# Half-token units and four PSUM sets in the up-projection of a GeGLU kernel

## The chip, the cores and the metric

The kernel runs on one core of a Trainium2 chip. The metric is the device time of one execution in microseconds: the median of six runs is 316.26 us, with runs from 314.55 to 317.0 us. A profile of one further execution shows where its time goes.

## What is computed

The input x has 32 x 32 = 1024 tokens of 1024 numbers; w_gate and w_up are 1024 x 3584, w_down is 3584 x 1024; all are bf16.

```
def _gelu(x):
    return jax.nn.gelu(x, approximate=True)

def reference(x, w_gate, w_up, w_down):
    return (_gelu(x @ w_gate) * (x @ w_up)) @ w_down
```

## The kernel before

The program is written engine by engine, with explicit semaphores. Each function (prog_sp, prog_act, prog_pool, prog_pe, prog_dve) is the instruction list of one engine in its order. `wait(clock, value)` makes an engine wait until another engine or a DMA has counted up to a value; a wait that is already known to hold is left out. The lists are written by hand; nothing plans or reorders them.

**Up-projection.** The 3584 hidden columns are 28 chunks m of 128. For each chunk TensorE forms the gate product G and the up product U for all 1024 tokens, hidden columns on the partitions: 2 products x 2 token halves h (512 tokens each) x 8 steps dk over the 1024 input columns, 32 matmuls of 128x128 by 128x512 (L292). The eight PSUM banks are two sets of four: two banks for G, two for U; chunk m uses set m % 2 (L287). A set is free again when D3 of chunk m - 2 is done (L274). Normally the order is G h0, G h1, U h0, U h1. For chunk 0 alone the order follows the arrival of x (L275 to L280): for each piece of x the four G steps and the four U steps that it allows.

**Between the two projections.** ScalarE and VectorE work a chunk of 1024 tokens at a time: A1 (L334) squares G into t; D1 (L352) forms i = (t + 1) * G; A2 (L337) takes the sigmoid of i; D2 (L357) multiplies it by U; D3 (L360) multiplies by G and writes hT, in bf16, to SBUF. D2 waits for the end of U. t, i and the result of D2 have two buffers each.

**Down-projection.** For each of 8 token blocks tc and two column halves dh TensorE sums 28 matmuls over m in one bank (L313). dh = 0 is copied out by ScalarE (L343), dh = 1 by VectorE (L366), and SP stores each block (L251).

**Loads.** x arrives transposed: SP issues four DMA transposes (L230), of 512 tokens by 512 columns each, in the order (h, q2) = (0,0), (0,1), (1,0), (1,1). The weights w_gate and w_up come in groups of chunks of sizes 1, 1, 2, 3, 4, 4, 4, 4, 4, 1, into two buffers each (wg0, wg1, wu0, wu1). The queues are:

- ACT issues wg of groups 0 and 1, behind one small activation that loads its table (L323, L326).
- POOL issues all wu loads (L217): those of groups 0 and 1 at once, those of groups 2 and 3 as soon as the transposed piece (0,1) has landed, the later ones when the chunk that last used the buffer has been read.
- SP issues wg from group 2 on (L242), behind its four transposes, the later ones with the same waits.
- wd arrives in seven groups of four chunks, by turns from SP and POOL (L201), each behind the G of a given chunk.

TensorE waits for wg and wu of a group at the group's first chunk, and within chunk 0 for the piece of x that a matmul reads (L289). Ahead of chunk 0 it runs eight dummy matmuls on a memset tile (L263).

Of the kernel before, what the change touches and what calls it, by code (L numbers as in the profile page):

```python
# [6 lines left out]
P = 128  # L7
BF16 = mybir.dt.bfloat16
FP32 = mybir.dt.float32
ACTF = mybir.ActivationFunctionType  # L10
ALU = mybir.AluOpType
# [77 lines left out]
def bass_standalone__geglu_ffn__sampling_kernel(  # L89
# [46 lines left out]
    NWB = 2  # L136
# [3 lines left out]
    wd_gate_chunk = [min(FM - 1, 3 + 3 * k) for k in range(len(wd_groups))]  # L140

# [9 lines left out]
    Q_X = {(h, q2): _Clock(f"x{h}{q2}", 16) for h in range(2) for q2 in range(2)}  # L151
# [10 lines left out]
    with ExitStack() as es:  # L162
# [8 lines left out]
        t_bufs = [sb("tb0", [P, N], FP32), sb("tb1", [P, N], FP32)]  # L171
        i_bufs = [sb("ib0", [P, N], FP32), sb("ib1", [P, N], FP32)]
        su_bufs = [sb("sb0", [P, N], FP32), sb("sb1", [P, N], FP32)]
# [8 lines left out]
        def g_full(s):  # L182
            return ps[:, 4 * s:4 * s + 2, :].rearrange("p a b -> p (a b)")

        def u_full(s):
            return ps[:, 4 * s + 2:4 * s + 4, :].rearrange("p a b -> p (a b)")
# [9 lines left out]
        def issue_wd(ew, eng, mine, upto_chunk, clock, force=False):  # L196
            for k in list(mine):
                if force or wd_gate_chunk[k] <= upto_chunk:
                    ew.wait(C_PE, ctx.get(("G", wd_gate_chunk[k])))
                    a, b = wd_groups[k]  # L200
                    ew.do(lambda: eng.dma_start(wd[:, a:b, :], wd_r[:, a:b, :]), clock=clock)  # L201
                    mine.remove(k)

        def prog_pool(eng):
            pool = _Eng(ctx, eng, C_POOL)
            ctx.set("scr", pool.do(lambda: eng.memset(osb[:, 0, 0:512], 1.0)))  # L206
            wd_mine = [k for k in range(len(wd_groups)) if k % 2 == 1]
            known_chunk = -1
            for j in range(NG):
                c0, gsz, buf, slot0 = groups[j]  # L210
                if j == 2:
                    pool.wait(Q_X[(0, 1)], ctx.get(("x", 0, 1)))
                if group_war[j] is not None:
                    pool.wait(C_PE, ctx.get(("U", group_war[j])))
                    known_chunk = max(known_chunk, group_war[j])
                ctx.set(("wu", j), pool.do(
                    lambda: eng.dma_start(wdst(wu_bufs, j), wsrc(wu_r, j)),  # L217
                    clock=Q_WU[j]))
                if j >= 2:
                    issue_wd(pool, eng, wd_mine, known_chunk, Q_WD_POOL)  # L220
            issue_wd(pool, eng, wd_mine, FM, Q_WD_POOL, force=True)
            ctx.set("wd_pool_total", Q_WD_POOL.n)

        XPIECES = [(0, 0), (0, 1), (1, 0), (1, 1)]

        def prog_sp(eng):
            sp = _Eng(ctx, eng, None)
            for (h, q2) in XPIECES:
                ctx.set(("x", h, q2), sp.do(
                    lambda: eng.dma_start_transpose(  # L230
                        xT[:, 4 * q2:4 * q2 + 4, h * 512:(h + 1) * 512],
                        xf[h * 512:(h + 1) * 512, q2 * 512:(q2 + 1) * 512],
                    ), clock=Q_X[(h, q2)]))
            wd_mine = [k for k in range(len(wd_groups)) if k % 2 == 0]
            known_chunk = -1
            for j in range(2, NG):
                c0, gsz, buf, slot0 = groups[j]
                if group_war[j] is not None:
                    sp.wait(C_PE, ctx.get(("U", group_war[j])))
                    known_chunk = max(known_chunk, group_war[j])  # L240
                ctx.set(("wg", j), sp.do(
                    lambda: eng.dma_start(wdst(wg_bufs, j), wsrc(wg_r, j)),  # L242
                    clock=Q_WG[j]))
                issue_wd(sp, eng, wd_mine, known_chunk, Q_WD_SP)
            issue_wd(sp, eng, wd_mine, FM, Q_WD_SP, force=True)
            ctx.set("wd_sp_total", Q_WD_SP.n)
            last = None
            for tc in range(TC):
                for dh in range(DH):
                    sp.wait(C_ACT if dh == 0 else C_DVE, ctx.get(("E", tc, dh)))  # L250
                    last = sp.do(lambda: eng.dma_start(  # L251
                        out_r[:, tc, dh * 512:(dh + 1) * 512],
                        osb[:, tc, dh * 512:(dh + 1) * 512]), clock=Q_OUT)
            sp.wait(Q_OUT, last)

        NDUMMY = 8

        def prog_pe(eng):
# [6 lines left out]
            ctx.set("dummy", v)  # L265
            pe.wait(C_PE, v)
            for m in range(FM):
                j, buf, slot = chunk_info[m]
                s = m % 2
                if m == groups[j][0]:  # L270
                    pe.wait(Q_WG[j], ctx.get(("wg", j)))
                    pe.wait(Q_WU[j], ctx.get(("wu", j)))
                if m >= 2:
                    pe.wait(C_DVE, ctx.get(("D3", m - 2)))  # L274
                if m == 0:  # L275
                    order = []
                    for (h, q2) in XPIECES:
                        for key in ("G", "U"):
                            for dk in range(4 * q2, 4 * q2 + 4):
                                order.append((key, h, dk))  # L280
                else:
                    order = [(key, h, dk) for key in ("G", "U") for h in range(NH)
                             for dk in range(DK)]
                cnt = {"G": 0, "U": 0}
                for (key, h, dk) in order:
                    wb = (wg_bufs if key == "G" else wu_bufs)[buf]
                    bank = 4 * s + (0 if key == "G" else 2) + h  # L287
                    if m == 0:
                        pe.wait(Q_X[(h, dk // 4)], ctx.get(("x", h, dk // 4)))  # L289
                    cnt[key] += 1  # L290
                    last = (cnt[key] == NH * DK)
                    v = pe.do(lambda: eng.matmul(  # L292
                        ps[:, bank, :],
                        wb[:, dk, slot * P:(slot + 1) * P],
                        xT[:, dk, h * 512:(h + 1) * 512],
                        start=(dk == 0), stop=(dk == DK - 1),
                    ), mark=last)
                    if last:
                        ctx.set((key, m), v)
            pe.wait(C_DVE, ctx.get(("D3", FM - 2)))  # L300
            pe.wait(Q_WD_SP, ctx.get("wd_sp_total"))
            pe.wait(Q_WD_POOL, ctx.get("wd_pool_total"))
            for tc in range(TC):
                for dh in range(DH):
                    b = (tc % 4) * 2 + dh
                    if tc >= 4:
                        pe.wait(C_ACT if dh == 0 else C_DVE, ctx.get(("E", tc - 4, dh)))
                    v = None
                    for m in range(FM):
                        if m == FM - 1:  # L310
                            pe.wait(C_DVE, ctx.get(("D3", FM - 1)))
# [9 lines left out]
        def prog_act(eng):  # L321
            act = _Eng(ctx, eng, C_ACT)
            act.do(lambda: eng.activation(warm[:, 0:1], const0, ACTF.Sigmoid))  # L323
            for j in range(2):
                ctx.set(("wg", j), act.do(
                    lambda: eng.dma_start(wdst(wg_bufs, j), wsrc(wg_r, j)),  # L326
                    clock=Q_WG[j]))
            for m in range(FM):
                s = m % 2
                tb, ib = t_bufs[m % 2], i_bufs[m % 2]  # L330
                act.wait(C_PE, ctx.get(("G", m)))
                if m >= 2:
                    act.wait(C_DVE, ctx.get(("D2", m - 2)))
                ctx.set(("A1", m), act.do(lambda: eng.activation(  # L334
                    tb[:, :], g_full(s), ACTF.Square, scale=SQ_SCALE)))
                act.wait(C_DVE, ctx.get(("D1", m)))
                ctx.set(("A2", m), act.do(lambda: eng.activation(  # L337
                    tb[:, :], ib[:, :], ACTF.Sigmoid, scale=SIG_SCALE)))
# [7 lines left out]
        def prog_dve(eng):  # L346
            dve = _Eng(ctx, eng, C_DVE)
            for m in range(FM):
                s = m % 2
                tb, ib, sub = t_bufs[m % 2], i_bufs[m % 2], su_bufs[m % 2]  # L350
                dve.wait(C_ACT, ctx.get(("A1", m)))
                ctx.set(("D1", m), dve.do(lambda: eng.scalar_tensor_tensor(  # L352
                    out=ib[:, :], in0=tb[:, :], scalar=1.0, in1=g_full(s),
                    op0=ALU.add, op1=ALU.mult)))
                dve.wait(C_ACT, ctx.get(("A2", m)))
                dve.wait(C_PE, ctx.get(("U", m)))
                ctx.set(("D2", m), dve.do(lambda: eng.tensor_tensor(  # L357
                    sub[:, :], tb[:, :], u_full(s), ALU.mult)))
                dve.wait(C_DVE, ctx.get(("D2", m)))
                ctx.set(("D3", m), dve.do(lambda: eng.tensor_tensor(  # L360
                    hT[:, m, :], sub[:, :], g_full(s), ALU.mult)))
# [57 lines left out]
```

## Time and profile before

| | us |
|---|---|
| median of six runs | 316.26 |
| the profiled execution, whole | 312.07 |
| its span, first to last instruction | 310.3 |
| TensorE busy with matmuls | 297.6 |
| VectorE busy | 108.1 |
| ScalarE busy | 64.5 |

The span is the time from the first to the last instruction of the profiled execution; the execution's own time has 1.77 us around that. The page has rows of 40 slices, each 7.76 us long: a digit is the busy share of an engine in tenths, and PEclk the granted clock of TensorE in tenths. A line of the chain gives the start, the length and what the chain runs through. A line of a group gives, behind the bar, the busy time and the mean ns of one instruction, then the idle time ahead of it and what ended it. Matmuls are pipelined, so a group's length on TensorE is somewhat more than the distance to the next group's start; the distance of starts is what one uses for the cost of a matmul.

### The profile page before, as it was taken

To read this page: it belongs to the slowest core of one execution; us is meant where nothing else is said; L and a number is where in the kernel's file an instruction comes from. 1 tells how busy PE (TensorE), PEld (TensorE's weight loads), DVE (VectorE), ACT (ScalarE), POOL (GpSimd) and SP (SyncE) were. 2 spreads that over 40 slices of the span, in tenths; PEclk is the share of its full clock that TensorE was granted. 3 is DMA by queue.
4 is the path that set the end of the run, shared out by engine and by line. 5 is a ranking of instruction groups with operands and counts; after the bars stand their busy time and mean duration, and the time that the engine had idled before them with its cause. 6 is when DMAs were issued, how large, how long until landed. Compare 5 with 4: busy or idle time off the path is not lost.

```text
span 310.3 us, 2978 instructions
## 1 busy us (share of the span) xinstructions
PE 297.6 (96%) x1352; PEld 133.3 (43%) x1352; DVE 108.1 (35%) x92; ACT 64.5 (21%) x66; POOL 12.0 (4%) x18
## 2 busy tenths in 40 slices
PE   4759999999999999999999999999999999999996
PEld 1224444444444444444444444444444444444442
DVE  0006555445545555455455554553000000000000
ACT  1013222233232222332332223321000000000000
POOL 3200010020001002000200100000000000000000
PEclk9589999999999999999999999999999999999999
DMA  7991009138008302900780150000100010010001
GB/s 169 219 302 53 2 3 346 59 112 293 0 2 271 135 2 62 343 2 2 226 316 2 28 174 0 2 0 0 35 18 17 17 36 17 17 35 18 17 17 34
DMA packets 25900, 26.40 MB, mean 85 GB/s; under 512 B 12080, under 2 KB 21296, under 8 KB 25888
## 3 DMA queue, kind: packets, MB, share of 16 engines
q1 hardware_dynamic: 21056, 15.21, 16.8%
q0 software_dynamic: 2752, 10.49, 9.9%
q10 hardware_dynamic: 2080, 0.52, 0.8%
q8 instruction: 10, 0.16, 0.2%
q14 instruction: 2, 0.02, 0.0%
HBM read 22.02 MB, written 2.10 MB: 78 GB/s over the span
## 4 chain that ended last, share of the span: by engine, by line
PE 92%; SPq 4%; DMA 3%; DVE 0%; issue 0%
PE ps L292 61%; PE ps L313 31%; SPq L230 4%; DMA xT<-in_x_dram 3%; DVE osb L366 0%
## 5 line engine op out<-in xcount | busy, mean ns | idle before, releaser
L292 PE MATMUL ps<-xT,wg 128*128 128x512 bf16 x448 | 104.1, 385 | 8.5 <-DMA wu<-in_w_up_dram 5.1
L292 PE MATMUL ps<-xT,wu 128*128 128x512 bf16 x448 | 103.5, 384 | 0.0
L313 PE MATMUL ps<-wd,hT 128*128 128x512 bf16 x448 | 96.9, 379 | 0.0
L292 PEld LDWEIGHTS ps<-xT,wg 128*128 128x128 bf16 x448 | 44.2, 99 | 63.5 <-issue 8.4
L292 PEld LDWEIGHTS ps<-xT,wu 128*128 128x128 bf16 x448 | 44.3, 99 | 54.2 <-issue 2.5
L313 PEld LDWEIGHTS ps<-wd,hT 128*128 128x128 bf16 x448 | 43.8, 98 | 52.9
L352 DVE SCALAR_TENSOR_TENSOR ib<-tb,ps 128x1024 f32<-128x1024 f32 x28 | 34.2, 1222 | 75.0 <-ACT tb L334 75.0
L334 ACT ACTIVATE tb<-ps 128x1024 f32<-128x1024 f32 x28 | 28.7, 1024 | 114.1 <-PE ps L292 114.1
L357 DVE TENSOR_TENSOR sb<-tb,ps 128x1024 f32<-128x1024 f32 x28 | 34.2, 1221 | 34.8 <-PE ps L292 33.6
L337 ACT ACTIVATE tb<-ib 128x1024 f32<-128x1024 f32 x28 | 29.6, 1057 | 36.1 <-DVE ib L352 36.1
L366 DVE CAST osb<-ps 128x512 bf16<-128x512 f32 x8 | 5.5, 692 | 89.3 <-PE ps L313 89.3
L360 DVE TENSOR_TENSOR hT<-sb,ps 128x1024 bf16<-128x1024 f32 x28 | 34.2, 1221 | 1.0
L343 ACT ACTIVATE osb<-ps 128x512 bf16<-128x512 f32 x8 | 4.8, 597 | 86.6 <-PE ps L313 86.6
L217 POOL DMA_DIRECT2D wu<-in_w_up_dram x10 | 9.0, 900 | 164.9 <-PE ps L292 155.5
L263 PE MATMUL ps<-osb 128*128 128x512 bf16 x8 | 3.2, 578 | 1.3 <-POOL osb L206 1.3
L263 PEld LDWEIGHTS ps<-osb 128*128 128x128 bf16 x8 | 1.0, 141 | 3.0 <-issue 1.7
L201 POOL DMA_DIRECT2D wd<-in_w_down_dram x3 | 2.3, 762 | 0.0
L323 ACT ACT_TABLE_LOAD x1 | 1.3, 1283 | 0.7 <-PEq L404 0.7
L206 POOL MEMSET osb<- 128x512 bf16 x1 | 0.5, 525 | 0.3 <-POOLq L404 0.3
L323 ACT ACTIVATE warm<-const-float32-0.0 128x1 f32<-128x1 f32 x1 | 0.2, 203 | 0.0
L404 POOL MEMSET const-float32-0.0<- 128x1 f32 x1 | 0.1, 99 | 0.2 <-issue 0.2
L404 POOL MEMSET const-float32-1.0<- 128x1 f32 x1 | 0.1, 99 | 0.0
(2 smaller groups left out, 0.2 us busy)
## 6 DMA issues: line engine op xcount, KB each, us to landing
wg<-in_w_gate_dram SPq DMA_DIRECT2D x5, 1024.0 KB, 5.4
wu<-in_w_up_dram POOLq DMA_DIRECT2D x5, 1024.0 KB, 10.0
wd<-in_w_down_dram SPq DMA_DIRECT2D x4, 1024.0 KB, 10.9
wd<-in_w_down_dram POOLq DMA_DIRECT2D x3, 1024.0 KB, 10.8
out_dram<-osb SPq DMA_DIRECT2D x16, 128.0 KB, 1.7
wu<-in_w_up_dram POOLq DMA_DIRECT2D x3, 256.0 KB, 7.8
wu<-in_w_up_dram POOLq DMA_DIRECT2D x1, 768.0 KB, 8.2
wg<-in_w_gate_dram SPq DMA_DIRECT2D x1, 768.0 KB, 10.4
```

What stands on the lines that cost most here:

```text
L217: lambda: eng.dma_start(wdst(wu_bufs, j), wsrc(wu_r, j)),
L230: lambda: eng.dma_start_transpose(xT[:, 4 * q2:4 * q2 + 4, h * 512:(h + 1) * 512], xf[h * 512:(h + 1) * 512, q2 * 512:(q2 + 1) * 512],), c ...
L263: v = pe.do(lambda: eng.matmul(ps[:, 7, :], osb[:, 0, 0:P], osb[:, 0, 0:512], start=True, stop=True), mark=(i == NDUMMY - 1))
L292: v = pe.do(lambda: eng.matmul(ps[:, bank, :], wb[:, dk, slot * P:(slot + 1) * P], xT[:, dk, h * 512:(h + 1) * 512], start=(dk == 0), stop ...
L313: v = pe.do(lambda: eng.matmul(ps[:, b, :], hT[:, m, tc * P:(tc + 1) * P], wd[:, m, dh * 512:(dh + 1) * 512], start=(m == 0), stop=(m == F ...
L334: ctx.set(("A1", m), act.do(lambda: eng.activation(tb[:, :], g_full(s), ACTF.Square, scale=SQ_SCALE)))
L337: ctx.set(("A2", m), act.do(lambda: eng.activation(tb[:, :], ib[:, :], ACTF.Sigmoid, scale=SIG_SCALE)))
L343: ctx.set(("E", tc, dh), act.do(lambda: eng.activation(osb[:, tc, dh * 512:(dh + 1) * 512], ps[:, b, :], ACTF.Copy)))
L352: ctx.set(("D1", m), dve.do(lambda: eng.scalar_tensor_tensor(out=ib[:, :], in0=tb[:, :], scalar=1.0, in1=g_full(s), op0=ALU.add, op1=ALU.m ...
L357: ctx.set(("D2", m), dve.do(lambda: eng.tensor_tensor(sub[:, :], tb[:, :], u_full(s), ALU.mult)))
L360: ctx.set(("D3", m), dve.do(lambda: eng.tensor_tensor(hT[:, m, :], sub[:, :], g_full(s), ALU.mult)))
L366: ctx.set(("E", tc, dh), dve.do(lambda: eng.tensor_copy(osb[:, tc, dh * 512:(dh + 1) * 512], ps[:, b, :])))
```

## The change

The unit of work in the up-projection becomes one chunk for one token half, written (m, h), with 16 matmuls. The order of units is (0,0), (1,0), (0,1), (1,1), then h = 0 and h = 1 of each further chunk. The eight PSUM banks become four sets of two, one bank for G and one for U; unit u uses set u % 4 and waits for D3 of the unit four before it. ScalarE and VectorE work unit by unit, on 512 tokens, with four buffers each for t, i and the result of D2, each 512 wide. The x transposes become eight pieces of 512 tokens by 256 columns, and chunks 0 and 1 both follow the pieces. The loads of groups 0 to 3 change their queues: ACT issues wg0, wu0, wg1, wu1; SP issues wg2, wu2, wg3, wu3 behind a wait for the last piece of x; POOL begins with group 4. The waits of the wd loads are for the end of U in place of G. In the down-projection each block waits for the last unit of its bank's set and, chunk by chunk, for D3 of the second token half. There are seven dummy matmuls in place of eight. The diff, with the parts that only rename left out:

```diff
+    NXQ = 4
+    QW = DK // NXQ
+    XPIECES = [(h, q2) for h in range(NH) for q2 in range(NXQ)]
+
+    units = [(0, 0), (1, 0), (0, 1), (1, 1)]
+    for m in range(2, FM):
+        for h in range(NH):
+            units.append((m, h))
+    NU = len(units)
+    NSETS = 4
...
+        NTB = 4
+        t_bufs = [sb(f"tb{i}", [P, 512], FP32) for i in range(NTB)]
+        i_bufs = [sb(f"ib{i}", [P, 512], FP32) for i in range(NTB)]
+        su_bufs = [sb(f"sb{i}", [P, 512], FP32) for i in range(NTB)]
...
+        def gbank(u):
+            return 2 * (u % NSETS)
+
+        def ubank(u):
+            return 2 * (u % NSETS) + 1
...
-                    ew.wait(C_PE, ctx.get(("G", wd_gate_chunk[k])))
+                    ew.wait(C_PE, ctx.get(("U", wd_gate_chunk[k], 1)))
...
+        def load_w(ew, eng, which, j):
+            if which == "wg":
+                return ctx.set(("wg", j), ew.do(
+                    lambda: eng.dma_start(wdst(wg_bufs, j), wsrc(wg_r, j)), clock=Q_WG[j]))
+            return ctx.set(("wu", j), ew.do(
+                lambda: eng.dma_start(wdst(wu_bufs, j), wsrc(wu_r, j)), clock=Q_WU[j]))
 
         def prog_pool(eng):
...
-            for j in range(NG):
...
-                if j == 2:
-                    pool.wait(Q_X[(0, 1)], ctx.get(("x", 0, 1)))
+            for j in range(4, NG):
...
         def prog_sp(eng):
...
-                        xT[:, 4 * q2:4 * q2 + 4, h * 512:(h + 1) * 512],
-                        xf[h * 512:(h + 1) * 512, q2 * 512:(q2 + 1) * 512],
+                        xT[:, QW * q2:QW * (q2 + 1), h * 512:(h + 1) * 512],
+                        xf[h * 512:(h + 1) * 512, QW * P * q2:QW * P * (q2 + 1)],
                     ), clock=Q_X[(h, q2)]))
+            sp.wait(Q_X[XPIECES[-1]], ctx.get(("x",) + XPIECES[-1]))
+            for j in (2, 3):
+                assert group_war[j] is None
+                load_w(sp, eng, "wg", j)
+                load_w(sp, eng, "wu", j)
...
-        NDUMMY = 8
+        NDUMMY = 7
 
         def prog_pe(eng):
...
-            for m in range(FM):
+            for u, (m, h) in enumerate(units):
                 j, buf, slot = chunk_info[m]
-                s = m % 2
-                if m == groups[j][0]:
-                    pe.wait(Q_WG[j], ctx.get(("wg", j)))
-                    pe.wait(Q_WU[j], ctx.get(("wu", j)))
-                if m >= 2:
-                    pe.wait(C_DVE, ctx.get(("D3", m - 2)))
...
+                pe.wait(Q_WG[j], ctx.get(("wg", j)))
+                pe.wait(Q_WU[j], ctx.get(("wu", j)))
+                if u >= NSETS:
+                    pm, ph = units[u - NSETS]
+                    pe.wait(C_DVE, ctx.get(("D3", pm, ph)))
+                if m < 2:
+                    order = [(key, dk) for q2 in range(NXQ) for key in ("G", "U")
+                             for dk in range(QW * q2, QW * (q2 + 1))]
                 else:
...
+                    order = [(key, dk) for key in ("G", "U") for dk in range(DK)]
...
-            pe.wait(C_DVE, ctx.get(("D3", FM - 2)))
...
-                    if tc >= 4:
+                    if tc < 4:
+                        ul = max(uu for uu in range(NU) if uu % NSETS == b // 2)
+                        pe.wait(C_DVE, ctx.get(("D3",) + units[ul]))
+                    else:
...
-                        if m == FM - 1:
-                            pe.wait(C_DVE, ctx.get(("D3", FM - 1)))
+                        pe.wait(C_DVE, ctx.get(("D3", m, 1)))
...
         def prog_act(eng):
...
             for j in range(2):
-                ctx.set(("wg", j), act.do(
-                    lambda: eng.dma_start(wdst(wg_bufs, j), wsrc(wg_r, j)),
-                    clock=Q_WG[j]))
...
+                load_w(act, eng, "wg", j)
+                load_w(act, eng, "wu", j)
```

## The prediction

> **What bounds the kernel now.** I read the two busy rows of the page first, then the chain that ended last in order of time.
>
> ```profile
> span 310.3 us, 2978 instructions
> ...
> PE   4759999999999999999999999999999999999996
> ...
> PEclk9589999999999999999999999999999999999999
> ```
> ```profile
> 2.24 7.70 SPq L230
> ...
> 12.06 8.54 DMA xT<-in_x_dram
> 20.60 0.04 issue
> 20.64 190.07 PE ps L292 x872
> 210.71 96.71 PE ps L313 x448
> ```
>
> From 20.64 us on the chain is TensorE and nothing else: 190.07 / 872 = 0.218 us per matmul, then 96.71 / 448 = 0.216. In the stretches by stage from 36 to 276 us PE is busy all the time, with 187 matmuls per 40 us (0.214 each) and a granted clock of 1.00. No stage in the middle has anything to give. What there is lies before 21 us, so I read the waits of PE, then its matmuls from 8 us in order of time (start, length of the group):
>
> ```profile
> PE ps L292 <- DMA wu<-in_w_up_dram: 5.1, 1, 5.1
> PE ps L292 <- DMA xT<-in_x_dram: 3.4, 1, 3.4
> ```
> ```profile
> 9.68 1.87 PE L292 MATMUL ps<-xT,wg 128*128 128x512 bf16 x4 [5.14 <-DMA wu<-in_w_up_dram]
> 11.34 1.91 PE L292 MATMUL ps<-xT,wu 128*128 128x512 bf16 x4
> ...
> 20.64 1.49 PE L292 MATMUL ps<-xT,wg 128*128 128x512 bf16 x4 [3.38 <-DMA xT<-in_x_dram]
> 21.93 1.91 PE L292 MATMUL ps<-xT,wu 128*128 128x512 bf16 x4
> 23.64 4.05 PE L292 MATMUL ps<-xT,wg 128*128 128x512 bf16 x16
> 27.52 3.62 PE L292 MATMUL ps<-xT,wu 128*128 128x512 bf16 x16
> 30.98 1.24 PE L292 MATMUL ps<-xT,wg 128*128 128x512 bf16 x5
> ```
>
> The first 64 matmuls (chunks 0 and 1) end at 30.98 us. At 0.216 they are 13.8 us of work. The rest is 9.68 us of waiting for wu, 3.38 us for x, and matmuls at 0.43 us (clock 0.50 from 7.44 to 14.2 us, and again from 21.0 to 24.45 us, after the wait for x). So **30.98 us is the mark**: everything behind it takes 279.3 us of span and, I argue below, stays. Why do wu and x come late? The DMA queues from 7 to 9 us and from 16 to 20 us (packets, MB, share of 16 engines):
>
> ```profile
> q0 software_dynamic: 115, 0.41, 103.0%
> q1 hardware_dynamic: 27, 0.00, 1.4%
> ```
> ```profile
> q0 software_dynamic: 288, 1.19, 101.3%
> q1 hardware_dynamic: 100, 0.03, 4.2%
> ```
>
> q0 carries POOL's wu loads, q1 SP's transposes and loads, q10 ACT's loads. A transpose of one piece (512 tokens by 512 columns) is 2080 packets (q1 moves 6178 between 9 and 16 us, three pieces). The first piece has all but some 30 of its packets through by 6.7 us, yet lands at 9.15 (issue 0.75 plus 8.4); the last has all but 32 through by 16.1 and lands at 20.60. In both stretches POOL's large packets hold the engines while the last packets of a transpose trickle.
>
> **The change, part by part.**
>
> *The wu loads of groups 0 and 1 go from POOL to ACT's queue.* ACT now issues wg0, wu0, wg1, wu1. Its two issues took 0.42 and 0.61 us, so four take about 2; one that blocks could take up to the 7.70 us of SP's second transpose. Queued behind them is ACT's first Square, not wanted before some 12 us, and with four PSUM sets TensorE needs its product only for the fifth unit, past 23 us: I take nothing. In q10 wg0's packets ran from 1.9 to 4.15 us, wg1's from 5.0 to 7.0, landing at 7.86. The second load is now wu0: t0 = 7.5 us, a little sooner than wg1 because nothing of POOL's is in the way, against 9.68. Here a rule speaks against the change: the Trainium skill, "DMA: Bandwidth & Descriptors", section "Issuing engines are not separate DMA queues", says that transfers from any issuer end on the same 16 engines, and another issuer only saves its issue time. By the rule wu0 would still land near 9.5 and t0 gain nothing; by the rows above, the queue decides who moves: q10 and q1 share evenly (741 and 928 packets from 5.0 to 6.5 us) where q0 leaves q1 27. I take the rows. wg1 and wu1, at about 2.1 us each with the 0.85 us gap seen between wg0 and wg1, end at 9.9 and 12.9, and wu1 lands at 13.2 us.
>
> *x in eight pieces of 1040 packets instead of four of 2080.* Bytes are the same. Between pieces the DMA share falls for some 0.5 us (11.3 to 11.9, 13.6 to 14.3), so four more borders cost about 0.4 us each if nothing fills them, 0 if q10 does. Bounds: 0, or that each piece takes as long as a whole one did (first rival). By 5.0 us q1 had moved 1090 packets, so x(0,0) lands near 5.5. From there q1 gets some 560 to 620 per us beside q10 and 890 alone (6178 in 7 us): 8320 in all by 15, and x(1,3) lands at 15.5 us (14.5 to 18).
>
> *Groups 2 and 3 go to SP, behind a wait for the last x piece.* Behind that wait on SP are only these four loads. wg2 and wu2 are 1 MB: from 15.5, 2.2 us to the first packet (0.75 to 3.0 for the first transpose), 1 MB at 307 GB/s (1.23 MB in the 4 us from 20.5) 3.4 us, 0.5 us to land: 21.6 us. Group 3, 1.5 MB, follows by 27 and is wanted 27 us after t0. POOL has no load left until chunk 3 ends, as before.
>
> *Units.* Order (0,0), (1,0), (0,1), (1,1): the second token half is first wanted at the third unit. Unit (0,0) runs cold as in the row of 9.68: some 10 matmuls by 0.428 and 6 by 0.216, 5.6 us, from 7.5 to 13.1. It needs x(0,3) by about 11.5; that is q1's packet 4160, near 10. Unit (1,0) waits for wu1, 13.2. Then three units of 16 x 0.216 = 3.45 us: 16.7, 20.1, 23.6. Unit (0,1) needs x(1,3) at 19. Unit (2,0) has group 2 from 21.6, so 2 us of cover; if x(1,3) is later than 17.5, the end moves with it. If the clock has not yet fallen at t0, unit (0,0) ends sooner and wu1 still sets 13.2: the sum hardly depends on it. **New mark 23.6 us, 7.4 before the old one.** One dummy matmul less (578 ns a row) ends at 4.1 instead of 4.5, hidden by the wait to 7.5.
>
> *Halved ACT and DVE work.* 56 units have three DVE operations and two ACT ones each. The wide ones took 1.22 and 1.02 to 1.06 us; the nearest rows at 512 wide are the evictions:
>
> ```profile
> L366 DVE CAST osb<-ps 128x512 bf16<-128x512 f32 x8 | 5.5, 692 | 89.3 <-PE ps L313 89.3
> ...
> L343 ACT ACTIVATE osb<-ps 128x512 bf16<-128x512 f32 x8 | 4.8, 597 | 86.6 <-PE ps L313 86.6
> ```
>
> DVE is then busy 3 x 0.69 = 2.08 us per 3.45 us unit, ACT 1.2. The ring through both (D1, A2, D2, D3, back to D1) is 0.69 + 0.60 + 0.69 + 0.69 plus hops of some 0.05 = 2.85 us: below 3.45. Bounds for one operation: 0.61 (half of 1.22) and 1.22 (no saving); I take 0.69. TensorE waits for D3 of four units back, over 10 us old. Cost and gain in the middle: 0, below too, since PE has no idle time there.
>
> A second rule: "TensorE: Matmul & The Clock Gate", section "A second HAM failure mode: psum-queue depth-cycling", says that at bf16 N=512 cycling through PSUM banks can idle TensorE enough that its clock swings. The change cycles units twice as often. By the rule, half clock in a tenth of the 193 us would cost 19 us; by the row, PE goes to a new bank every 8 matmuls already, with PEclk at 9 in every slice. I take 0.
>
> *The hand-over to the down projection.* Unit 52's D3 is over 6 us old when tc 0 begins; the last D3 comes about 1.5 us after the last matmul and is wanted by matmul 28, 6 us in. 0. The wd loads wait for U instead of G, 3.5 us later at most, with tens of us of cover. The tail (0.69 us eviction, then the store) stays.
>
> **Sum.** Span 310.3 - 7.4 = 302.9; the profiled execution took 312.07, so 304.7 there. The median of the runs shown, 316.26, is 4.2 above that execution, and the trace doesn't tell where. I carry the saving over: 308.9 us.
>
> **The rivals.**
>
> *Pieces cost by instruction.* Three pieces took 7.1 us (9.0 to 16.1), 2.35 each. If half pieces take that too: 3.0 + 8 x 2.35 = 21.8, landing 22.3; group 2 at 28.4. TensorE stands for almost 5 us, the clock falls (as after 3.38 us in the row of 20.64), 1.7 us more: gain about 0.9, 315.4 us. Against it: q1 at 112% of the engines' share from 9 to 16 us; packets fill the time, not issues.
>
> *ACT's queue is slow beside the transposes.* With 3.5 us per load, wu1 lands at 16.2: 3 us of the gain go, 312 us.
>
> *Slower: the ACT-DVE ring becomes the bound.* Place: every unit. The ring decides from the point where its four operations together pass 3.3 us, that is 72% of their wide price (3 x 1.22 + 1.06 = 4.72). At 75% it takes 3.69, 0.24 over, times 52 units = 12.5, less 7.4: 321.4 us. For it: fixed costs per operation double in number. Against: 692 and 597 are 57% of the wide ones.
>
> **Chances.** Forecast 0.72 (307 to 311), slow ACT queue or late group 2 0.10 (311 to 313.5), pieces by instruction 0.07 (315.4), ring or clock 0.06 (321), and 0.05 for more (304 to 306.5), if part of the 4.2 us is a longer start. Half a per cent, 1.6 us, is about what a measurement of this kernel can tell from no change. Faster 0.87, same 0.07, slower 0.06. The range 306.0 to 312.5 leaves out the two rivals of no gain and the tails.
>
> **What would show it.** The first matmul of chunk 0 near 7.5 us and the start of chunk 2 near 23.6; one cold stretch instead of two; no q0 packets before 30 us; x landed near 15.5; 512-wide operations near 0.69 and 0.60; no PE idle time past 24 us. Wrong if PE waits for wg or wu at unit (2,0), or shows a gap at each unit.

## The result, and the profile after

The changed kernel takes 304.71 us (median of 10, 304.13 to 306.37) against 314.72 us for the kernel before (median of 20, 311.56 to 317.0). The ratio is 0.972, with a 95% interval of 0.969 to 0.975; like every ratio below it leaves out executions of a kernel that lie over 1.5% above its fastest one, which is why it is nearer to 1 than the ratio of the medians, 0.968, for medians and spreads count every execution. The forecast was 308.9 us, between 306.0 and 312.5: the sign was right and so, in the main, was the mechanism; the time lies below the range.

The profiled execution took 304.59 us, its span is 302.8 us. The forecast for these two, made from the trace alone, was 304.7 and 302.9. So the sum over the trace held to 0.1 us, in part by luck as told below, and the miss is in the step from the one traced execution to the median. The rows of 40 slices of the page after:

```profile
span 302.8 us, 3148 instructions
...
PE   4999999999999999999999999999999999999996
...
PEclk9799999999999999999999999999999999999999
```

The second and third slices, at 7 and 5 before, are full, and the second drop of the clock is gone. TensorE's matmuls in order of time, after the change:

```profile
7.64 0.86 PE L298 MATMUL ps<-xT,wg 128*128 128x512 bf16 x2 [3.15 <-DMA wu<-in_w_up_dram]
...
11.42 0.60 PE L298 MATMUL ps<-xT,wg 128*128 128x512 bf16 x2 [0.35 <-DMA xT<-in_x_dram]
...
23.51 1.89 PE L298 MATMUL ps<-xT,wg 128*128 128x512 bf16 x8
```

The row of 23.51 is the first group of eight, the start of chunk 2 and the mark of the prediction (30.98 before, 23.6 forecast). Behind it lie 302.8 - 23.51 = 279.3 us, as before. The wait for x shrank from 3.38 to 0.35 us; it is now for the third piece. POOL's queue moves no packet before 36 us. ACT's and SP's queues from 4.5 to 6.5 us, ahead of that wait:

```profile
q10 hardware_dynamic: 1652, 0.42, 125.2%
q1 hardware_dynamic: 157, 0.03, 9.4%
```

The halved operations are the rows of VectorE and ScalarE:

```profile
L360 DVE SCALAR_TENSOR_TENSOR ib<-tb,ps 128x512 f32<-128x512 f32 x56 | 38.5, 687 | 48.7 <-ACT tb L341 48.6
L341 ACT ACTIVATE tb<-ps 128x512 f32<-128x512 f32 x56 | 33.4, 597 | 89.9 <-PE ps L298 89.9
```

0.69 and 0.60 us, as taken (the sigmoid took 0.63). They cost 12.8 us more of VectorE and 10.4 more of ScalarE than before (120.9 and 74.9 us busy), and none of it reaches TensorE.

### The profile page after: what moved, and what is told of

Same layout as the page of the kernel before. It is cut to its first block, busy times and chain, and to the rows that moved or that the text cites. A ratio compares the mean times of both kernels' runs of the same rounds, so it can differ in the third digit from the quotient of the medians.

```text
span 302.8 us, 3148 instructions
## 1 busy us (share of the span) xinstructions
PE 295.1 (97%) x1351; PEld 132.4 (44%) x1351; DVE 120.9 (40%) x176; ACT 74.9 (25%) x122; POOL 8.4 (3%) x14
## 4 chain that ended last, share of the span: by engine, by line
PE 95%; DMA 2%; SPq 1%; DVE 0%; issue 0%
PE ps L298 63%; PE ps L320 32%; DMA xT<-in_x_dram 2%; SPq L240 1%; DVE osb L374 0%
## 5 line engine op out<-in xcount | busy, mean ns | idle before, releaser
L298 PE MATMUL ps<-xT,wg 128*128 128x512 bf16 x448 | 108.5, 381 | 3.5 <-DMA wu<-in_w_up_dram 3.1
L298 PE MATMUL ps<-xT,wu 128*128 128x512 bf16 x448 | 108.7, 381 | 0.0
L360 DVE SCALAR_TENSOR_TENSOR ib<-tb,ps 128x512 f32<-128x512 f32 x56 | 38.5, 687 | 48.7 <-ACT tb L341 48.6
L341 ACT ACTIVATE tb<-ps 128x512 f32<-128x512 f32 x56 | 33.4, 597 | 89.9 <-PE ps L298 89.9
L365 DVE TENSOR_TENSOR sb<-tb,ps 128x512 f32<-128x512 f32 x56 | 38.5, 688 | 39.0 <-ACT tb L344 39.0
L344 ACT ACTIVATE tb<-ib 128x512 f32<-128x512 f32 x56 | 35.2, 629 | 42.7 <-DVE ib L360 42.7
L368 DVE TENSOR_TENSOR hT<-sb,ps 128x512 bf16<-128x512 f32 x56 | 38.5, 687 | 1.9
L220 POOL DMA_DIRECT2D wu<-in_w_up_dram x6 | 5.5, 910 | 160.9 <-PE ps L298 160.9
## 6 DMA issues: line engine op xcount, KB each, us to landing
wd<-in_w_down_dram POOLq DMA_DIRECT2D x3, 1024.0 KB, 10.4
```

The lines of the kernel that those rows point to most:

```text
L220: lambda: eng.dma_start(wdst(wu_bufs, j), wsrc(wu_r, j)), clock=Q_WU[j]))
L298: v = pe.do(lambda: eng.matmul(ps[:, bank, :], wb[:, dk, slot * P:(slot + 1) * P], xT[:, dk, h * 512:(h + 1) * 512], start=(dk == 0), stop ...
L341: ctx.set(("A1", m, h), act.do(lambda: eng.activation(tb[:, :], gb, ACTF.Square, scale=SQ_SCALE)))
L344: ctx.set(("A2", m, h), act.do(lambda: eng.activation(tb[:, :], ib[:, :], ACTF.Sigmoid, scale=SIG_SCALE)))
L360: ctx.set(("D1", m, h), dve.do(lambda: eng.scalar_tensor_tensor(out=ib[:, :], in0=tb[:, :], scalar=1.0, in1=gb, op0=ALU.add, op1=ALU.mult)))
L365: ctx.set(("D2", m, h), dve.do(lambda: eng.tensor_tensor(sub[:, :], tb[:, :], ubk, ALU.mult)))
```

## The experiments

Two questions were open: where before loses more than its trace shows, and which part of the change (the units and PSUM sets, the eight pieces, the two moves of loads) brings the gain. All runs but one were timed in five rounds beside the kernel before; "spread" is the highest execution less the lowest, and "mark" the start of chunk 2 in the profile. In every trace of this study the span less the mark is 279.3 us to within 0.1, so the mark alone tells where a kernel stands.

| kernel | median us (n) | spread | mark | ratio to before, 95% |
|---|---|---|---|---|
| before, beside the next four rows | 315.97 (17) | 6.8 | 30.98 in the first trace | 1 |
| before, POOL behind the last piece | 306.90 (6) | 0.8 | 25.45 | 0.976 (0.972 to 0.981) |
| before, wu0 and wu1 on ACT | 308.99 (6) | 3.2 | 26.43 | 0.983 (0.977 to 0.988) |
| before, both | 305.64 (6) | 0.4 | 24.70 | 0.973 (0.969 to 0.977) |
| units with old loads and pieces | 314.09 (12) | 6.9 | 31.89 | 0.995 (0.990 to 1.000) |
| before, beside the next four rows | 315.20 (23) | 8.7 | | 1 |
| after, wu0 and wu1 on POOL | 307.24 (6) | 1.8 | 25.64 | 0.984 (0.977 to 0.991) |
| after, groups 2, 3 as before | 314.66 (12) | 2.9 | 34.10 | 1.008 (1.003 to 1.012) |
| after, four pieces | 305.90 (6) | 1.3 | 25.42 | 0.979 (0.973 to 0.985) |
| before, wu0 to wu3 on ACT | 311.25 (12) | 2.7 | 28.68 | 0.995 (0.990 to 0.999) |

**1. Before, with POOL's groups 2 and 3 behind the last piece of x.**

```diff
                 if j == 2:
-                    pool.wait(Q_X[(0, 1)], ctx.get(("x", 0, 1)))
+                    pool.wait(Q_X[(1, 1)], ctx.get(("x", 1, 1)))
```

> The kernel before, with one wait changed: POOL sends wu of groups 2 and 3 when the last transposed piece (1,1) has landed, not after (0,1). Theory S (a transpose's last packets are held up by another queue's traffic, POOL's above all, by an amount that differs from execution to execution; this is where before loses both the 7.4 us in its profile and the further 2 to 4 us of its median): no q0 packets from 12.5 to 16.5 us, piece (1,1) lands near 16.6 in place of 20.6, no wait of 3.4 us and no second cold stretch; chunk 2 starts near 25.9 in place of 30.98, span near 305.2, time near 307; executions lie closer together than those of before (5.4 us from lowest to highest in 20). Rival C (before's executions differ by how long TensorE's clock stays at half): the cold stretch at the start stays, the spread shrinks only by the part of the second stretch, and time follows the mean clock of each execution. Rival N (the spread comes from nothing at the start): the saving is 5 us in the median too, the spread stays at 5.

Measured: 306.90 us, span 304.7, mark 25.45. The matmuls of chunk 0 no longer wait for the second token half; those of the second half start at 14.97 and 16.80:

```profile
14.97 1.03 PE L292 MATMUL ps<-xT,wg 128*128 128x512 bf16 x4
...
16.80 1.04 PE L292 MATMUL ps<-xT,wg 128*128 128x512 bf16 x4
```

One argument changed, and 9.1 us of the median go (about 7.4 by the ratio), where the span fell by 5.6. The spread falls from 6.8 to 0.8 us. So what no first trace showed, 3.5 us by the medians, goes with the same wait: this rules out rival N. Against rival C, this kernel's first matmuls still come 0.43 us apart, as those of before do, and at the same mean clock the two kernels lie 6 to 8 us apart: four executions of this one at 0.988 took 306.87 to 307.27 us, five of before beside it at 0.989 took 313.23 to 314.75.

**2. Before, with wu of groups 0 and 1 on ACT.**

```diff
-            for j in range(NG):                 # POOL
+            for j in range(2, NG):
...
             for j in range(2):                  # ACT, behind its wg load
+                ctx.set(("wu", j), act.do(
+                    lambda: eng.dma_start(wdst(wu_bufs, j), wsrc(wu_r, j)), clock=Q_WU[j]))
```

> The kernel before, with wu of groups 0 and 1 sent by ACT in place of POOL; POOL begins with group 2 behind piece (0,1). Theory S: first matmul at 7.6 in place of 9.68, piece (0,1) lands sooner, so POOL's groups 2 and 3 start sooner and hold up pieces (1,0) and (1,1): (1,1) lands between 18 and 20.6; chunk 2 starts between 28 and 30.5, span 307.5 to 310; the executions stay as widely spread as before, since the wait for (1,1) behind POOL's packets stays. Rival C: the same time, but a spread that goes with the clock.

Measured: 308.99 us, span 305.7, mark 26.43: a larger gain than theory S had, since piece (1,1) had landed at 17.75 in this trace, below the range expected. The spread was expected to stay; it is 3.2 us, half of before's. Which execution one traces matters here too: the traced one, 307.53, is among the best of the six.

**3. Before, with both edits.**

> The kernel before with both edits of the queues: wu of groups 0 and 1 from ACT, wu of groups 2 and 3 on POOL behind the last piece (1,1). Units, PSUM sets and the four pieces stay as before. Theory S: no q0 packets until the last piece has landed; first matmul at 7.6, (1,1) landed near 15.5, chunk 2 starts near 24.1 to 25, span 303.5 to 304.5, time 305.5 to 306.5, and a spread of 2 us or so like that of after: nearly all of the change's gain without its units. Rival U (the half-token units bring the gain): the span stays above 307.

Measured: 305.64 us, span 304.0, mark 24.70, spread 0.4. The start of chunk 2, in one group of sixteen as before:

```profile
24.70 3.62 PE L292 MATMUL ps<-xT,wg 128*128 128x512 bf16 x16
```

With whole-chunk work, two PSUM sets and four pieces, two edits of the queues take 10.3 of the 315.97 us. Rival U falls. The two gains don't add: alone the edits took 9.1 and 7.0.

**4. The units alone.** The changed kernel with the old queues, the old waits of the loads, and NXQ = 2.

```diff
-    NXQ = 4
+    NXQ = 2
...
-            for j in range(4, NG):              # POOL
+            for j in range(NG):
+                if j == 2:
+                    pool.wait(Q_X[(0, NXQ - 1)], ctx.get(("x", 0, NXQ - 1)))
...
-                load_w(act, eng, "wu", j)
...
-            sp.wait(Q_X[XPIECES[-1]], ctx.get(("x",) + XPIECES[-1]))
             for j in (2, 3):
...
                 load_w(sp, eng, "wg", j)
-                load_w(sp, eng, "wu", j)
```

> The changed kernel with the old queues and four pieces: wu of groups 0 to 3 on POOL with the old waits, wg of groups 2 and 3 on SP at once; half-token units and four PSUM sets stay. Theory S: first matmul at 9.65, unit (1,0) fills the wait for the second token half until 18.9; piece (1,1) lands near 20.6 as in before and the mark (start of chunk 2) is near 25.8, span near 305; but the executions stay widely spread, since (1,1)'s landing sets the mark: median 2 us or more above its own profiled execution. Rival U: 304 to 305 us with the narrow spread of after. Rival C: a single cold stretch, so the narrow spread of after.

Measured: 314.09 us, span 311.2, spread 6.9; the interval of the ratio touches 1. The wide spread came as theory S has it, the span didn't: 305 was expected. The row of the second half shows why:

```profile
19.91 1.03 PE L298 MATMUL ps<-xT,wu 128*128 128x512 bf16 x4
25.01 0.88 PE L298 MATMUL ps<-xT,wg 128*128 128x512 bf16 x2 [4.07 <-DMA xT<-in_x_dram]
```

Unit (1,0) and the first half of (0,1) cover the time to 20.94, but the last piece lands at 24.96 us. The same loads, with the same waits on POOL, gave 20.60 in the trace of before. Its DMA queues from 15.5 to 23 us, in packets, MB and share:

```profile
q0 software_dynamic: 238, 0.96, 77.3%
q1 hardware_dynamic: 563, 0.15, 30.6%
```

POOL's transfer is itself slow here (0.96 MB in 7.5 us; before it moved 1.19 in 4), and the piece waits for all of it. The units shift work in front of the wait, and the wait is longer than what they shift.

**5. Before once more, in another execution.**

> The kernel before, unchanged, profiled in another execution. Theory S: piece (1,1) lands at another time than 20.60 us, by up to some microseconds, and the span differs from 310.3 by about as much as chunk 2's start differs from 30.98; the stretch behind it takes 279.3 us again. Rival N: the stretch behind chunk 2's start differs. Rival C: landings within 0.5 us of the first trace, and only the stretches of half clock differ.

Measured: 312.79 us, span 311.0, mark 31.70. From its chain and its matmuls in order of time:

```profile
11.93 9.64 DMA xT<-in_x_dram
```
```profile
21.62 1.89 PE L292 MATMUL ps<-xT,wg 128*128 128x512 bf16 x4 [4.42 <-DMA xT<-in_x_dram]
```

The last piece lands at 21.57, 0.97 us later than in the first trace; the start of chunk 2 and the span move by 0.7, and 311.0 - 31.70 is again 279.3. Both traced executions of before are good ones, though: none at its median, near 315, has been traced. That the landing moves by several microseconds in those is inferred from runs 1, 3 and 4. A lower mean clock goes with a longer time: over the 40 timed executions of before beside the runs of 1 to 4 and 6 to 9, those at a mean clock of 0.989 have a median near 314 and those at 0.978 near 316. It doesn't fix the time, though: the executions at 0.984 lie between 312.80 and 318.83. And it can be a result of the wait as well as a cause: in both traces the clock is at half after the wait for the last piece (from 21.0 to 24.5 us in the first).

**6. After, with wu of groups 0 and 1 back on POOL.** In the diff of the change, ACT's `load_w(act, eng, "wu", j)` goes to the head of POOL's list, for j in (0, 1).

> The changed kernel with one load pair moved back: wu of groups 0 and 1 from POOL at the start, all else as changed. Theory S: POOL's packets again hold the first transposes' last packets and wu0 lands late; first matmul near 9.5 in place of 7.64; units (0,0) to (1,1) follow without further waits: 9.5 + 5.6 + 3 x 3.45, chunk 2 starts near 25.5 in place of 23.51; span near 304.8, time 306.5, spread about 2 us, since nothing of POOL's runs beside the later pieces. Rival (the gain at the start is the units'): 304.7 as changed.

Measured: 307.24 us, span 305.0, mark 25.64, spread 1.8. TensorE starts at 8.18, sooner than expected, and then waits 1.24 us for the second piece. The move of these two loads is worth 2.5 us by the medians, 2.1 by the marks.

**7. After, with groups 2 and 3 as before.** wu from POOL behind the last piece of the first token half, wg from SP without a wait; units, eight pieces and ACT's loads stay.

```diff
-            for j in range(4, NG):              # POOL
+            pool.wait(Q_X[(0, NXQ - 1)], ctx.get(("x", 0, NXQ - 1)))
+            for j in range(2, NG):
...
-            sp.wait(Q_X[XPIECES[-1]], ctx.get(("x",) + XPIECES[-1]))
             for j in (2, 3):
...
                 load_w(sp, eng, "wg", j)
-                load_w(sp, eng, "wu", j)
```

> The changed kernel with the loads of groups 2 and 3 as in the kernel before: wu from POOL as soon as the last piece of the first token half has landed, wg from SP without a wait. Theory S: POOL's packets hold the pieces of the second token half; the last lands between 18 and 26 us, by execution; chunk 2 starts between 25 and 31; median 307 to 312 and a spread of 4 to 6 us, against 2.2 for the changed kernel. Rival C (clock): one cold stretch only, so spread near 2. Rival U (units hide it): time within 1 us of 304.7.

Measured: 314.66 us, with 315.20 for before beside it (ratio 1.008), mark 34.10: later than the range expected, with a spread of 2.9, less than expected. All else of the change stands, and none of its gain is left.

```profile
21.62 0.59 PE L296 MATMUL ps<-xT,wu 128*128 128x512 bf16 x2
28.01 1.03 PE L296 MATMUL ps<-xT,wg 128*128 128x512 bf16 x2 [5.79 <-DMA xT<-in_x_dram]
```

Four waits for x, 10.5 us together. With the same loads, four pieces and whole chunks took 308.99 us (run 2). Why this is worse isn't shown, since units and pieces weren't parted here. What the trace shows is that two landings were held, not one: the seventh piece had all but 32 of its packets through by 14.4 us and landed at 21.14, the eighth at 27.97.

**8. After, with four pieces** (NXQ = 2, nothing else).

> The changed kernel with four transposed pieces in place of eight. Theory S: pieces decide little: first matmul at 8.0 as in the kernel before with both queue edits, second piece near 11.8, chunk 2 starts near 24.4, 0.9 us later than as changed; span 303.7, time 305.5, narrow spread. If the finer pieces mattered much: 307 or more.

Measured: 305.90 us, span 304.7, mark 25.42, spread 1.3. The finer pieces are worth 1.2 us by the medians and 1.9 by the traces, of which this one is the slowest of its six; the two kernels were timed apart, and the intervals of their ratios, 0.973 to 0.985 and 0.969 to 0.975, overlap. With four pieces, units (this run) and whole chunks (run 3) give 305.90 and 305.64. The loads of the two keep clear of the transposes, but aren't quite the same: in run 3 wu of groups 2 and 3 comes from POOL, and their wg from SP without a wait. So half-token units and four PSUM sets are worth nothing that these runs can tell. Whole chunks with eight pieces weren't run.

**9. Before, with wu of groups 0 to 3 on ACT, without a wait.** As run 2, with groups 2 and 3 of wu behind the others in ACT's list.

> The kernel before with wu of groups 0 to 3 all sent by ACT, at once and without a wait; POOL begins with group 4. It asks whether it is POOL's queue that holds the transposes, or any other queue that is busy beside them. If POOL's alone: ACT's and SP's packets share evenly, piece (1,1) lands at 17 to 18.5, chunk 2 starts at 26 to 27.5, span 305.5 to 307, spread 2 us or less. If any queue: (1,1) lands at 20 or later, chunk 2 starts at 29.5 or later, span 309 or more, and the spread is wide (4 us or more).

Measured: 311.25 us, span 308.0, mark 28.68, spread 2.7: between the two cases, nearer to "any queue". TensorE's waits for x and ACT's queue from 11 to 13 us:

```profile
14.16 1.89 PE L289 MATMUL ps<-xT,wg 128*128 128x512 bf16 x4 [2.21 <-DMA xT<-in_x_dram]
...
18.31 1.04 PE L289 MATMUL ps<-xT,wg 128*128 128x512 bf16 x4 [0.91 <-DMA xT<-in_x_dram]
```
```profile
q10 hardware_dynamic: 1143, 0.55, 120.9%
```

In these 2 us no packet of SP's queue is recorded. Piece (0,1) has its data through by about 10.5 us and lands at 14.1, after two of ACT's loads. So it isn't POOL's alone: in this trace too a transpose lands only after the loads of another queue that run beside its end. With ACT's loads beside them the executions lie within 2.7 us, with POOL's (before, beside the same runs) within 8.7.

**10. After, with 16 dummy matmuls in place of 7.**

> The changed kernel with 16 dummy matmuls in place of 7. It asks what sets the mark now. If it is the landing of x and wu1, as the wait of the changed profile at 11.42 says, a warm clock at the first matmul buys little: unit (0,0) waits for its third piece until 11.4 all the same, and chunk 2 starts at 23.2 to 23.5; 304.4 to 304.8. If it is the cold clock: up to 2 us less, 302.8.

Measured: 304.27 us (6 executions, 304.04 to 306.19), mark 23.18. At full clock from the first matmul on, TensorE waits for the third piece until 11.08: a warm clock has little to save (0.33 us of the mark), as the landing of x is the limit.

**11 and 12. Group 1 behind the fourth piece.** wg1 and wu1 from SP after piece (0,3), not from ACT; in run 12 also 16 dummy matmuls.

> The changed kernel with wg and wu of group 1 sent by SP behind the fourth piece of x, not by ACT beside the pieces. Theory S: nothing but wg0 and wu0 runs beside the first four pieces, so they land by about 9.5; unit (0,0) no longer waits at 11.4; with its cold clock it still ends near 13, wu1 lands near 12, chunk 2 starts near 23.2: 304.4, within 0.5 us of the changed kernel. If a single queue serves slower: 305.5 or more.

> The kernel with group 1 behind the fourth piece on SP and 16 dummy matmuls: both limits of the start at once. Unit (0,0) runs from 7.6 to 11.1 at full clock, unit (1,0) waits for wu1 until about 12, chunk 2 starts near 22.4: 303.6, 1 us below the changed kernel. If the dummies still run cold when the loads are in (16 x 0.43 = 6.9 us, to 8.2), 304.5.

Measured: 304.57 (304.30 to 304.86) and 304.56 us (304.31 to 305.02), spans 302.5 and 302.8. In both, the clock was at full rate from the first matmul on, and the four pieces land sooner; yet unit (1,0) waits for wu1 until 12.42 and 12.50, in run 11:

```profile
12.42 0.59 PE L301 MATMUL ps<-xT,wg 128*128 128x512 bf16 x2 [1.63 <-DMA wu<-in_w_up_dram]
```

Unit (2,0) starts 0.3 and 0.45 us late, at 23.24 and 23.47, as wu of group 2 lands at 23.15 and 23.38. SP sends group 2 only behind the last piece, at 17.33 and 17.61, against 16.79 in the changed kernel: what the first half gains, group 2 gives back. None of the three can be told from 304.71.

## Why the prediction was right or wrong

- **The step that failed: the base.** The prediction noted that before's median, 316.26, was 4.2 us above its traced execution, and said "I carry the saving over: 308.9 us". That takes the 4.2 us as something that both kernels have. Measured, after's median is 0.1 us above its traced execution, and this alone put the time outside the range. Two things were in the 4.2. Some 1.5 came from the sample of six: over 20 executions before's median is 314.72, and the saving carried over from there would have given 307.3, within the range. The other 2.65 was part of what the change removes. Run 1 shows where it sat: holding back POOL's loads until the last piece has landed takes 9.1 us off the median and 5.6 off the span. The last case of the chances (0.05, "if part of the 4.2 us is a longer start") is what happened.
- **The mark: right in number, 23.6 against 23.51, in part by luck (next point).** The first matmul came at 7.64 (7.5 forecast), unit (0,0) ended at 13.15 (13.1), and one cold stretch was left.
- **What sets the mark: wrong, and two errors met.** The prediction had wu1 end the wait at 13.2, and expected q10 and q1 to share evenly, with x(0,3) landed near 10. From 4.5 to 6.5 us ACT's queue moved 1652 packets and SP's 157, x(0,3) landed at 12.01, and wu1, landed at 11.15, was never waited for. The third piece set the pace (runs 10 to 12). All but 32 of its packets had moved by 9.5 us, but it landed at 11.37, just behind wu1; with ACT's group 1 out of the way (run 11) it landed at 8.29. So ACT's loads now hold a transpose, as POOL's did. That unit (0,0) still ended as forecast comes from the cold matmuls ahead of that wait, which fill the same time.
- **Groups 2 and 3 on SP: right in effect, late in size.** SP's wait for the last piece ended at 16.79, where 15.5 was forecast for its landing, and wu of group 2 landed at 22.59 (21.6). TensorE didn't wait for it at 23.51, with 0.9 us of cover and not 2; in runs 11 and 12, with group 2 half a microsecond later and the units half a microsecond sooner, it did.
- **POOL's packets hold the transposes: right, and larger than summed.** Runs 1, 3, 4 and 7 show it from both sides. The sum had given it the 3.38 us of wait and the cold stretch of one trace.
- **The rule on issuing engines.** Run 6 puts the move of wu0 and wu1 from POOL to ACT at 2.5 us, with the first matmul 0.54 us later when they are moved back, and a further wait of 1.24. The rule of the Trainium skill, "DMA: Bandwidth & Descriptors", section "Issuing engines are not separate DMA queues", would have made that move worth the issue time alone. The measurement decides.
- **Halved operations, ring, clock in the middle: right.** 187 matmuls in every 40 us from 36 to 276 us and a clock of 1.00, as before. The swings that the Trainium skill, "TensorE: Matmul & The Clock Gate", section "A second HAM failure mode: psum-queue depth-cycling", describes for cycling PSUM banks are not seen here.
- **The rivals.** Pieces by instruction: no, the last four half pieces landed 1.0 to 1.4 us apart, where 2.35 was the price of a whole one. The last of eight landed at 16.77, though, and the last of four at 15.85 (run 8): the extra borders were not free. A slow ACT queue: ACT's loads were fast, it is SP's that stood aside. The ring: no.
- **Slips in the working that change nothing in the sum.** Of the 9.68 us put down to waiting for wu, 5.14 are that wait; the rest is the start and the dummy matmuls. PEclk is at 9 in every slice of before only from the fourth on (the second is 5). 3.3 of 4.72 us is 70%, not 72. Before's last piece had all but 32 of its packets through at 16.2 us, not 16.1.

Still open: why POOL's transfer beside the transposes takes 4 us in one execution and over 7 in another, and what holds a transpose's last packets. The traces show that they come late, not by what they are ordered.

## What to carry to other kernels

A change named for pipelining may get its gain from the queues that it moves on the way: take those edits alone first. Where the runs of a kernel lie some per cent apart and its trace is among the good ones, ask which wait could vary, and count the gap to the median to that wait before carrying a saving over. In this kernel it paid to keep other queues' loads back until the DMA transposes that compute waits for had landed, as long as the loads held back weren't themselves wanted next (runs 11 and 12).

## What the runs showed of the hardware

- A DMA transpose of 512 by 512 landed 4.4 us after all but its last 32 packets had moved (16.2 to 20.60 us in before, POOL's loads beside it); with POOL's loads held back (run 1) the same piece landed 0.8 us after (16.0 to 16.76). A piece of 512 by 256 took 6.7 us (14.4 to 21.14, run 7).
- Two queues of the same kind, SP's and ACT's, didn't share evenly: 157 against 1652 packets in 2 us (after), 0 against 1143 in another 2 (run 9). At other times it was the other way round: 799 against 22 in the microsecond from 8.0 (after).
- The clock: with 7 dummy matmuls ending near 4.5 us, first matmuls at 6.85 ran 0.215 us apart (run 11), and at 7.64 0.43 apart (after).
